# w2, dw2 and the MLP's inner columns on 128 partitions instead of 96

## The chip, the cores and the metric

One core of one Trainium2 chip runs the whole program. The metric is the device time of one execution in microseconds (us); fewer is better. Each comparison ran on one chip, with the kernel before timed in the same rounds. The span of a profile is some 2 us shorter than the time.

## The reference, cut to what matters

The program is a forward pass and its gradient. A gate mixes one decode step of attention with 32 heads over a cache of 4096 keys (A) and an MLP (B). The outputs are the mixed vector and the gradients of nine inputs; only the constant `B_x` gets none.

```python
D, H, Sk, Dh, F = 640, 32, 4096, 128, 1728          # all bfloat16

def _A_ref(x, k_cache, v_cache, wq, wo):
    q = ...(x @ wq)...
    scores = jnp.einsum("bhqd,bhkd->bhqk", q, k_cache) * (Dh ** -0.5)
    p = _softmax(scores, axis=-1)
    o = jnp.einsum("bhqk,bhkd->bhqd", p, v_cache)
    return ...(o)... @ wo

def _B_ref(x, w1, b1, w2):                          # w1 640x1728, w2 1728x640
    h = jnp.einsum("bsd,df->bsf", x, w1) + b1
    sp = jnp.log1p(jnp.exp(-jnp.abs(h))) + jnp.where(h > 0, h, jnp.zeros_like(h))
    act = h * jnp.tanh(sp)
    return jnp.einsum("bsf,fd->bsd", act, w2)

g = _sigmoid((x * gate_w).sum(-1, keepdims=True))
out = g * a + (1 - g) * b
# outputs: out, then the vector-Jacobian product with grad_out for
# x, k_cache, v_cache, wq, wo, w1, b1, w2, gate_w
```

K and V are 33.5 MB each, and so are their gradients. So some four fifths of the traffic (134 of 164.9 MB) are the caches coming in and their gradients going out. w2 is 2.2 MB, and dw2 goes out with as much.

## The kernel before: what the change and the argument touch

All loads but three small rows are issued by SyncE into one queue, and nearly all stores by GpSimd into another. w2 has 1728 rows. Before, each of 96 partitions holds 18 consecutive rows, and three loads bring six of the 18 each. The first two are issued with the loads of the start, and the third mid-run, when a buffer is free.

```python
    FP = 96
    FCN = F // FP            # 18
    FCC = 6
    NCH = FCN // FCC         # 3
    w2_v = B_w2.rearrange("(p fc) n -> p fc n", p=FP)
    dw2_v = out_8.rearrange("(p fc) n -> p fc n", p=FP)
    # ... cut
    def load_w2(c):
        w2cs[c] = mlp.tile([FP, FCC, D], BF16, name="w2c", tag="w2c", bufs=2)
        nc.sync.dma_start(w2cs[c][:], w2_v[:, c * FCC:(c + 1) * FCC, :])

    load_wq(0); load_wo(0); load_k(0); load_v(0); load_k(1); load_v(1); load_wo(1)   # (one per line there)
    nc.sync.dma_start(w1_sb[:], w1_v)
    # ... cut: b1
    load_k(2)
    load_v(2)
    load_w2(0)
    load_w2(1)
```

The work on w2 is one VectorE step for each of the 18 columns of rows in each direction (`dh_part`, `dw2_part`), and five small matmuls for each column for h and again for b:

```python
        def h_part(a, b):  # ... cut
                        nc.tensor.matmul(hps[a][:, fc:fc + 1],
                                         lhsT=w1_sb[:, rc, :].rearrange("p (q c) -> p q c", c=FCN)[:, :, fc],
                                         rhs=x_bf[:, rc:rc + 1], start=(rc == 0), stop=(rc == RC - 1))
        def dh_part(c, i):  # ... cut
                nc.vector.scalar_tensor_tensor(junk[0:FP, 0:D], in0=w2cs[c][:, i, :], scalar=m["dm"][:, fc:fc + 1],
                                               in1=db_bc[0:FP, :], op0=ALU.mult, op1=ALU.mult,
                                               accum_out=m["dh"][:, fc:fc + 1])
```

Two parts of the attention are used by experiments: the sum O over 32 tiles of V in each head, as 32 matmuls with their weight loads (dQ, with K, looks the same), and the last store of all:

```python
            for j in range(a, b):
                nc.tensor.matmul(O, lhsT=vts[h][:, j, :], rhs=st["e"][:, j:j + 1].to_broadcast([P, W]),
                                 start=(j == 0), stop=(j == J - 1))
    # ... cut
    nc.gpsimd.dma_start(dwq_v[:, :, CL:], dwq_l[:])
```

## Time and profile before

The kernel before took 414.11 us, the median of 3 runs (413.64 to 414.41).

| what | where it is read | value |
|---|---|---|
| span | page | 412.1 us |
| bytes moved | page, DMA packets | 164.93 MB |
| VectorE, TensorE busy | page, part 1 | 308.8 us (75%), 305.7 us (74%) |
| DMA in the steady stages | windows | 420 to 422 GB/s, share 1.01 |
| DMA from 28 to 36 us | windows | 291 GB/s, share 1.02 |
| one DMA engine alone at the end | windows | 400 to 408 us |

The windows say more. Each line is a stretch of the span, then its length, the busy time of PE, PEld, DVE, ACT and POOL with counts, then the granted clock, the DMA share and GB/s:

```profile
28.00:36.00 8.00, 7.01 (x165) 6.61 (x165) 5.96 (x14) 4.24 (x10) 1.20 (x2) 1.00 1.02 291
36.00:200.00 164.00, 143.09 (x2726) 132.15 (x2727) 130.04 (x352) 78.25 (x185) 18.27 (x34) 0.98 1.01 421
200.00:280.00 80.00, 55.61 (x1073) 50.08 (x1072) 57.94 (x148) 32.63 (x74) 8.08 (x15) 0.85 1.01 420
304.00:372.00 68.00, 56.36 (x1170) 50.57 (x1168) 61.17 (x150) 35.09 (x80) 10.70 (x17) 1.00 1.01 422
372.00:380.00 8.00, 5.84 (x134) 5.47 (x133) 7.62 (x14) 3.24 (x8) 3.04 (x4) 1.00 0.91 373
380.00:397.00 17.00, 3.42 (x65) 2.30 (x63) 14.85 (x47) 0.79 (x3) 4.73 (x8) 0.59 1.01 417
```

In the three steady stages (36 to 280 and 304 to 372 us) the DMA engines are busy all the time at 420 to 422 GB/s, while the load of the compute engines changes from stage to stage. From 28 to 36 us they are just as busy and move 30% less. The finer windows put this at 30 to 36 us, just where the two early w2 loads are in flight:

```profile
28.00:30.00 2.00, 2.00 (x55) 1.99 (x56) 1.48 (x3) 1.00 (x2) 0.34 (x1) 1.00 1.08 432
30.00:32.00 2.00, 1.47 (x26) 1.35 (x25) 0.55 (x2) 0.67 (x3) 0.32 (x1) 1.00 1.04 254
32.00:34.00 2.00, 1.96 (x38) 1.86 (x36) 2.00 (x3) 2.00 (x5) 0.00 (x0) 1.00 0.99 231
34.00:36.00 2.00, 1.59 (x58) 1.41 (x54) 1.93 (x8) 0.57 (x2) 0.53 (x1) 1.00 1.00 249
```

The end, again by windows, and the closing DRAIN of GpSimd's queue from the view of its source line (durations in ns as min/median/max, then first and last start):

```profile
397.00:400.00 3.00, 0.00 (x0) 0.00 (x0) 0.00 (x0) 0.00 (x0) 0.00 (x0) 0.50 0.76 311
400.00:402.00 2.00, 0.00 (x0) 0.00 (x0) 0.00 (x0) 0.00 (x0) 0.00 (x0) 0.50 0.06 24
404.00:406.00 2.00, 0.00 (x0) 0.00 (x0) 0.00 (x0) 0.00 (x0) 0.00 (x0) 0.50 0.06 27
...
L815 POOLq DRAIN  x3: 45/102/17857, 393.5 to 411.9; - x3
```

A share of 0.06 is one engine of 16. By the landings of the last store, fifteen have ended by 400.5 us and one ends at 407.9 us. The first DRAIN starts at 393.5 us and lasts 17.857 us, so it ends at 411.4 us, 3.5 us after the last store has landed.

### The profile page before, as it was taken

The page shows a single profiled execution, that of the slowest core. Times are in us where ns is not written, and L with a number is a line of the kernel's source. Part 1 is how long each engine was busy: PE and PEld are TensorE (multiplying, and loading weights), DVE is VectorE, ACT ScalarE, POOL GpSimd, SP SyncE. Part 2 cuts the span into 40 slices and gives each one's busy share as a digit, 9 for nine tenths or more (in the row PEclk, how much of TensorE's full clock was granted, in tenths as well). Part 3 has the DMA queues.
Part 4 walks back from the last instruction along what each step waited for, and adds up shares of the span by engine and source line. Part 5 has one row for each costly group of instructions (what it writes and reads, how often), then busy time and mean ns, then how long its engine had stood idle before and what let it go on. Part 6 is the DMA issues. An engine that isn't in the chain of part 4 may idle for free.

```text
span 412.1 us, 13687 instructions
## 1 busy us (share of the span) xinstructions
PE 305.7 (74%) x5916; PEld 277.5 (67%) x5916; DVE 308.8 (75%) x807; ACT 177.0 (43%) x410; POOL 49.9 (12%) x95
## 2 busy tenths in 40 slices
PE   0688899988998789898977688439888788886200
PEld 0577888888887678787867687428777678775200
DVE  3338655685679999999897688528999997978840
ACT  1354534434445455445534356305554555543000
POOL 0001001111110111121111112001111111133310
PEclk9998999999999999989996899958999999999555
DMA  8999999999999999999999999999999999999970
GB/s 292 421 405 336 421 425 415 421 423 425 420 426 422 423 411 415 424 421 422 427 411 425 423 421 419 420 424 393 407 401 428 422 422 421 422 423 383 421 313 14
DMA packets 26328, 164.93 MB, mean 400 GB/s; under 512 B 2812, under 2 KB 2812, under 8 KB 10012
## 3 DMA queue, kind: packets, MB, share of 16 engines
q1 hardware_dynamic: 14116, 82.03, 48.8%
q0 software_dynamic: 12112, 82.03, 47.8%
q8 instruction: 46, 0.75, 0.7%
q14 instruction: 14, 0.11, 0.1%
q10 hardware_dynamic: 40, 0.01, 0.0%
HBM read 82.03 MB, written 82.03 MB: 398 GB/s over the span
## 4 chain that ended last, share of the span: by engine, by line
DVE 33%; PE 30%; DMA 23%; ACT 7%; issue 3%; ACTq 0%; DVEq 0%
DMA Kn<-in_A_k_cache_dram 17%; PE tr L559 10%; DVE dK_sb L584 8%; DVE dV_sb L584 7%; DMA out_dram<-dK_sb 6%; ACT tT L561 6%; PE sA L628 4%; DVE junk L376 4%; PE sA L568 3%; PE h_ps L407 3%; PE sB L681 3%; DVE junk L279 2%; DVE junk L508 2%; PE sB L568 1%; DMA vec_rows<-in_gate_w_dram 1%
## 5 line engine op out<-in xcount | busy, mean ns | idle before, releaser
L561 ACT COPY tT<-tr 128x512 f32<-128x512 f32 x256 | 142.3, 587 | 140.9 <-PE tr L559 140.2
L568 PEld LDWEIGHTS <-tT 128*128 128x128 bf16 x2048 | 80.4, 98 | 40.3 <-ACT tT L561 34.9
L559 PE MATMUL tr<-ident_f,Kn 128*128 128x128 f32 x512 | 80.7, 295 | 6.5 <-DMA Kn<-in_A_k_cache_dram 6.5
L584 DVE TENSOR_TENSOR dV_sb<-p_bf,qd 128x2048 bf16<-128x2048 bf16 x64 | 77.9, 1218 | 2.8 <-DMA out_dram<-dK_sb 2.8
L584 DVE TENSOR_TENSOR dK_sb<-ds_bf,qd 128x2048 bf16<-128x2048 bf16 x64 | 77.7, 1215 | 0.0
L559 PE MATMUL tr<-ident_f,Vn 128*128 128x128 f32 x512 | 72.6, 277 | 0.1
L568 PE MATMUL sA<-qd,tT 128*128 128x48 bf16 x1024 | 48.8, 187 | 23.5 <-ACT dq_all L686 12.8
L559 PEld LDWEIGHTS tr<-ident_f,Kn 128*128 128x128 f32 x512 | 60.1, 150 | 7.6 <-issue 6.2
L559 PEld LDWEIGHTS tr<-ident_f,Vn 128*128 128x128 f32 x512 | 56.8, 143 | 0.2 <-PE sA L568 0.2
L568 PE MATMUL sB<-qd,tT 128*128 128x48 bf16 x1024 | 46.1, 183 | 0.1
L611 POOL DMA_DIRECT2D out_dram<-dV_sb x32 | 18.3, 572 | 166.8 <-DVE dV_sb L584 74.2
L628 PEld LDWEIGHTS <-Vn 128*128 128x128 bf16 x1024 | 30.2, 96 | 10.4 <-issue 10.4
L601 POOL DMA_DIRECT2D out_dram<-dK_sb x31 | 18.3, 591 | 151.0 <-DVE rz L650 77.7
L628 PE MATMUL sA<-e_bf,Vn 128*128 128x48 bf16 x1024 | 30.7, 183 | 7.6 <-DVE zs L648 6.0
L681 PE MATMUL sB<-ds_bf,Kn 128*128 128x48 bf16 x1024 | 31.8, 185 | 3.5 <-DVE ds_bf L670 3.5
L681 PEld LDWEIGHTS <-Kn 128*128 128x128 bf16 x1024 | 29.2, 97 | 3.8 <-issue 3.8
L632 DVE TENSOR_REDUCE m<-sA 128x1 f32<-128x32 f32 x32 | 6.0, 189 | 31.3 <-PE sA L568 25.6
L279 DVE SCALAR_TENSOR_TENSOR junk<-wo_g,da_bc 128x640 bf16<-128x640 bf16 x32 | 26.3, 821 | 2.6 <-ACT da_bc L220 1.1
L376 DVE SCALAR_TENSOR_TENSOR junk<-wq_g,dq_bc 128x1024 bf16<-128x1024 bf16 (+1 forms) x25 | 25.1, 1004 | 0.2
L668 DVE TENSOR_SCALAR_CACHE_REDUCE dj<-sB,rz 128x128 f32<-128x128 f32 x32 | 11.1, 346 | 11.2 <-PE sB L662 11.2
L407 PE MATMUL h_ps<-cols_bf,w_sb 128*96 128x1 bf16 x90 | 18.2, 313 | 1.4 <-ACT qd L290 0.7
L407 PEld LDWEIGHTS <-w_sb 128*96 128x96 bf16 x90 | 17.6, 272 | 1.8 <-issue 0.7
(144 smaller groups left out, 283.8 us busy)
## 6 DMA issues: line engine op xcount, KB each, us to landing
Kn<-in_A_k_cache_dram SPq DMA_DIRECT2D x32, 1024.0 KB, 27.2
Vn<-in_A_v_cache_dram SPq DMA_DIRECT2D x32, 1024.0 KB, 26.9
out_dram<-dV_sb POOLq DMA_DIRECT2D x32, 1024.0 KB, 12.2
out_dram<-dK_sb POOLq DMA_DIRECT2D x31, 1024.0 KB, 12.3
wq_g<-in_A_wq_dram SPq DMA_DIRECT2D x4, 1280.0 KB, 19.0
wo_g<-in_A_wo_dram SPq DMA_DIRECT2D x8, 640.0 KB, 13.3
out_dram<-wo_g POOLq DMA_DIRECT2D x8, 640.0 KB, 11.6
out_dram<-dwq_t POOLq DMA_DIRECT2D x5, 896.0 KB, 16.6
```

The source lines that it names most:

```text
L279: nc.vector.scalar_tensor_tensor(junk[:, 0:D], in0=wos[g][:, i, :], scalar=1.0, in1=da_bc[:], op0=ALU.mult, op1=ALU.mult, accum_out=gp["do ...
L376: nc.vector.scalar_tensor_tensor(junk[:, c0:c1], in0=wqs[w][:, rc, c0:c1], scalar=1.0, in1=dq_bc[:, w * WG * Dh + c0:w * WG * Dh + c1], op ...
L407: nc.tensor.matmul(hps[a][:, fc:fc + 1], lhsT=w1_sb[:, rc, :].rearrange("p (q c) -> p q c", c=FCN)[:, :, fc], rhs=x_bf[:, rc:rc + 1], star ...
L559: nc.tensor.transpose(tp[:, t, :], flat[:, k * P:(k + 1) * P], ident_f[:])
L561: nc.scalar.copy(sb[:].rearrange("p a b -> p (a b)"), tp[:].rearrange("p a b -> p (a b)"))
L568: nc.tensor.matmul(out[:, 2 * k:2 * k + W], lhsT=tb[:, t, par, :], rhs=vec[:, par, :].unsqueeze(1).to_broadcast([P, W // 2, 2]), start=(pa ...
L584: nc.vector.tensor_tensor(dst[:, a:b, :].rearrange("p j (a b) -> p j a b", b=2), col[:, a:b, :].unsqueeze(2).to_broadcast([P, n, Dh // 2, 2]),
L601: nc.gpsimd.dma_start(dKv[h], st["dK"][:])
L611: nc.gpsimd.dma_start(dVv[h], st["dV"][:])
L628: nc.tensor.matmul(O, lhsT=vts[h][:, j, :], rhs=st["e"][:, j:j + 1].to_broadcast([P, W]), start=(j == 0), stop=(j == J - 1))
L668: nc.vector.tensor_scalar(dj[:], PT, rz[:], None, ALU.mult, ALU.add, accum_out=dd[:])
L681: nc.tensor.matmul(DQ, lhsT=kts[h][:, j, :], rhs=ds[:, j, 0:1].to_broadcast([P, W]), start=(j == 0), stop=(j == J - 1))
```

## The change

The intent is to spread w2 and dw2 evenly. 13 rows go on each of 128 partitions (1664 rows), and the 64 rows left over go in a tile of 64 partitions. So 14 columns of work take the place of 18. The diff, cut to its core:

```diff
-    FP = 96
-    FCN = F // FP
-    FCC = 6
-    NCH = FCN // FCC
+    FM = F // P
+    FB = FM * P
+    FR = F - FB
+    FCN = FM + 1
+    CH = [(0, 5), (5, 9), (9, FCN)]
+    NCH = len(CH)
...
-    w2_v = B_w2.rearrange("(p fc) n -> p fc n", p=FP)
-    dw2_v = out_8.rearrange("(p fc) n -> p fc n", p=FP)
+    w2_v = B_w2[0:FB, :].rearrange("(p fc) n -> p fc n", p=P)
+    dw2_v = out_8[0:FB, :].rearrange("(p fc) n -> p fc n", p=P)
...
     def load_w2(c):
-        w2cs[c] = mlp.tile([FP, FCC, D], BF16, name="w2c", tag="w2c", bufs=2)
-        nc.sync.dma_start(w2cs[c][:], w2_v[:, c * FCC:(c + 1) * FCC, :])
+        a, b = CH[c][0], min(CH[c][1], FM)
+        w2cs[c] = mlp.tile([P, 5, D], BF16, name="w2c", tag="w2c", bufs=2)
+        nc.sync.dma_start(w2cs[c][:, 0:b - a, :], w2_v[:, a:b, :])
...
     load_w2(0)
+    w2r = mlp.tile([FR, D], BF16, name="w2r", tag="w2r")
+    nc.sync.dma_start(w2r[:], B_w2[FB:F, :])
     load_w2(1)
...
-                        nc.tensor.matmul(hps[a][:, fc:fc + 1],
-                                         lhsT=w1_sb[:, rc, :].rearrange("p (q c) -> p q c", c=FCN)[:, :, fc],
+                        w = (w1_sb[:, rc, 0:FB].rearrange("p (q c) -> p q c", c=FM)[:, :, fc] if fc < FM
+                             else w1_sb[:, rc, FB:F])
+                        nc.tensor.matmul(hps[a][0:rows(fc), fc:fc + 1], lhsT=w,
...
-    nc.sync.dma_start(out0_rows, fin_rows[0:RC, :])
-    nc.scalar.dma_start(out1_rows, fin_rows[RC:2 * RC, :])
-    nc.sync.dma_start(out9_rows, fin_rows[2 * RC:3 * RC, :])
+    for eng, dst, i, cut in ((nc.sync, out0_rows, 0, 4), (nc.scalar, out1_rows, 1, 3), (nc.sync, out9_rows, 2, 2)):
+        for a, b in ((0, cut), (cut, RC)):
+            eng.dma_start(dst[a:b, :], fin_rows[i * RC + a:i * RC + b, :])
```

Cut: the same split in the b, dh, dw2 and dh-broadcast steps, b1 as two loads, and db1 stored from the broadcast row.

More of the change, by code (lines that the diff above doesn't have):

```diff
@@ L60 @@
     assert Dh == P and J % 8 == 0 and D % P == 0 and H % WG == 0
-    assert F % FP == 0 and FCN % FCC == 0 and FCN % 2 == 0
+    assert 0 < FR <= P and FCN == 14
     Kv = A_k_cache.rearrange("b h (p j) d -> (b h) p j d", p=P)
@@ L72 @@
     dw1_v = out_6.rearrange("(rc r) f -> r rc f", r=P)
-    w2_v = B_w2.rearrange("(p fc) n -> p fc n", p=FP)
-    dw2_v = out_8.rearrange("(p fc) n -> p fc n", p=FP)
-    b1_v = B_b1.rearrange("(p fc) -> p fc", p=FP)
-    db1_v = out_7.rearrange("(p fc) -> p fc", p=FP)
+    w2_v = B_w2[0:FB, :].rearrange("(p fc) n -> p fc n", p=P)
+    dw2_v = out_8[0:FB, :].rearrange("(p fc) n -> p fc n", p=P)
+    b1_v = B_b1[0:FB].rearrange("(p fc) -> p fc", p=P)
     x_rows = A_x.rearrange("a b (c p) -> (a b c) p", p=P)
@@ L148 @@
     nc.sync.dma_start(w1_sb[:], w1_v)
-    b1c = const.tile([FP, FCN], BF16, name="b1c")
-    nc.sync.dma_start(b1c[:], b1_v)
+    b1c = const.tile([P, FCN], BF16, name="b1c")
+    nc.gpsimd.memset(b1c[:], 0.0)
+    nc.sync.dma_start(b1c[:, 0:FM], b1_v)
+    nc.sync.dma_start(b1c[0:FR, FM:FCN], B_b1[FB:F].rearrange("(p c) -> p c", c=1))
     load_k(2)
@@ L397, in mlp_steps, with rows, w2p @@
         m = {}
-        T = lambda name, dt=F32, shape=(FP, FCN): const.tile(list(shape), dt, name=name)
+        T = lambda name, dt=F32, shape=(P, FCN): const.tile(list(shape), dt, name=name)
         b1f = T("b1f")
         hps = {}
+        def rows(fc):
+            return P if fc < FM else FR
+        def w2p(fc):
+            c = [i for i in range(NCH) if CH[i][0] <= fc < CH[i][1]][0]
+            return w2cs[c][:, fc - CH[c][0], :] if fc < FM else w2r[:]
         def h_part(a, b):
             def f():
-                hps[a] = gr_ps.tile([FP, FCN], F32, name="h_ps", tag="gr")
+                hps[a] = gr_ps.tile([P, FCN], F32, name="h_ps", tag="gr")
                 for fc in range(a, b):
                     for rc in range(RC):
-                        nc.tensor.matmul(hps[a][:, fc:fc + 1],
-                                         lhsT=w1_sb[:, rc, :].rearrange("p (q c) -> p q c", c=FCN)[:, :, fc],
+                        w = (w1_sb[:, rc, 0:FB].rearrange("p (q c) -> p q c", c=FM)[:, :, fc] if fc < FM
+                             else w1_sb[:, rc, FB:F])
+                        nc.tensor.matmul(hps[a][0:rows(fc), fc:fc + 1], lhsT=w,
                                          rhs=x_bf[:, rc:rc + 1], start=(rc == 0), stop=(rc == RC - 1))
@@ L416, in f @@
                     m["h"] = T("h_sb")
-                nc.vector.tensor_tensor(m["h"][:, a:b], hps[a][:, a:b], b1f[:, a:b], ALU.add)
+                    nc.gpsimd.memset(m["h"][:], 0.0)
+                r = rows(a)
+                nc.vector.tensor_tensor(m["h"][0:r, a:b], hps[a][0:r, a:b], b1f[0:r, a:b], ALU.add)
             return f
@@ L421, in act1 @@
             h = m["h"]
-            ee = T("ee", shape=(FP, 2, FCN))
+            ee = T("ee", shape=(P, 2, FCN))
             nc.scalar.activation(ee[:, 0, :], h[:], ACT.Exp, scale=1.0)
             nc.scalar.activation(ee[:, 1, :], h[:], ACT.Exp, scale=-1.0)
-            e1 = T("e1", shape=(FP, 2, FCN))
+            e1 = T("e1", shape=(P, 2, FCN))
             nc.vector.tensor_scalar(e1[:], ee[:], 1.0, None, ALU.add)
-            sg = T("sg", shape=(FP, 2, FCN))
+            sg = T("sg", shape=(P, 2, FCN))
             nc.vector.reciprocal(sg[:], e1[:])
@@ L455, in act2 @@
             m["dh"] = T("dh32")
+            nc.gpsimd.memset(m["dh"][:], 0.0)
         def b_part(c):
@@ L460, in f @@
                 for n in range(RC):
-                    for i in range(FCC):
-                        nc.tensor.matmul(m["bp"][:, n:n + 1], lhsT=w2cs[c][:, i, n * P:(n + 1) * P],
-                                         rhs=m["act_bf"][:, c * FCC + i:c * FCC + i + 1],
-                                         start=(i == 0), stop=(i == FCC - 1))
+                    a, b = CH[c]
+                    for fc in range(a, b):
+                        nc.tensor.matmul(m["bp"][:, n:n + 1], lhsT=w2p(fc)[:, n * P:(n + 1) * P],
+                                         rhs=m["act_bf"][0:rows(fc), fc:fc + 1],
+                                         start=(fc == a), stop=(fc == b - 1))
             return f
@@ L468, in b_add, with dh_part, dw2_part @@
             nc.vector.tensor_tensor(b_acc[:], b_acc[:], m["bp"][:], ALU.add)
-        def dh_part(c, i):
+        def dh_part(fc):
             def f():
-                fc = c * FCC + i
-                nc.vector.scalar_tensor_tensor(junk[0:FP, 0:D], in0=w2cs[c][:, i, :], scalar=m["dm"][:, fc:fc + 1],
-                                               in1=db_bc[0:FP, :], op0=ALU.mult, op1=ALU.mult,
-                                               accum_out=m["dh"][:, fc:fc + 1])
+                r = rows(fc)
+                nc.vector.scalar_tensor_tensor(junk[0:r, 0:D], in0=w2p(fc), scalar=m["dm"][0:r, fc:fc + 1],
+                                               in1=db_bc[0:r, :], op0=ALU.mult, op1=ALU.mult,
+                                               accum_out=m["dh"][0:r, fc:fc + 1])
             return f
-        def dw2_part(c, i0, i1):
+        def dw2_part(c, f0, f1):
             def f():
-                for i in range(i0, i1):
-                    fc = c * FCC + i
-                    nc.vector.tensor_scalar(w2cs[c][:, i, :], db_bc[0:FP, :], m["act_f"][:, fc:fc + 1], None, ALU.mult)
-                if i1 == FCC:
-                    nc.gpsimd.dma_start(dw2_v[:, c * FCC:(c + 1) * FCC, :], w2cs[c][:])
+                for fc in range(f0, f1):
+                    r = rows(fc)
+                    nc.vector.tensor_scalar(w2p(fc), db_bc[0:r, :], m["act_f"][0:r, fc:fc + 1], None, ALU.mult)
+                if f1 == CH[c][1]:
+                    a, b = CH[c][0], min(f1, FM)
+                    nc.gpsimd.dma_start(dw2_v[:, a:b, :], w2cs[c][:, 0:b - a, :])
+                    if f1 == FCN:
+                        nc.gpsimd.dma_start(out_8[FB:F, :], w2r[:])
             return f
@@ L491, in dh_cast @@
             nc.vector.tensor_copy(m["dh_bf"][:], m["dh"][:])
-            nc.gpsimd.dma_start(db1_v, m["dh_bf"][:])
             m["dh_bc"] = mlp.tile([P, F], BF16, name="dh_bc", tag="dh_bc")
@@ L496, in f @@
             def f():
-                ps = gr_ps.tile([P, hc, FP], BF16, name="dhb_ps", tag="gr")
+                ps = gr_ps.tile([P, hc, P], BF16, name="dhb_ps", tag="gr")
                 for i in range(hc):
-                    nc.tensor.transpose(ps[:, i, :], m["dh_bf"][:, k * hc + i:k * hc + i + 1].to_broadcast([FP, P]),
-                                        ident_bf[0:FP, 0:FP])
-                nc.scalar.copy(m["dh_bc"][:].rearrange("p (q c) -> p q c", c=FCN)[:, :, k * hc:(k + 1) * hc],
-                               ps[:].rearrange("p c q -> p q c"))
+                    fc = k * hc + i
+                    r = rows(fc)
+                    nc.tensor.transpose(ps[:, i, 0:r], m["dh_bf"][0:r, fc:fc + 1].to_broadcast([r, P]),
+                                        ident_bf[0:r, 0:r])
+                n = min(hc, FM - k * hc)
+                nc.scalar.copy(m["dh_bc"][:, 0:FB].rearrange("p (q c) -> p q c", c=FM)[:, :, k * hc:k * hc + n],
+                               ps[:, 0:n, :].rearrange("p c q -> p q c"))
+                if k == 1:
+                    nc.scalar.copy(m["dh_bc"][:, FB:F], ps[:, n, 0:FR])
+                    nc.gpsimd.dma_start(out_7.rearrange("(o f) -> o f", o=1), m["dh_bc"][0:1, :])
             return f
@@ L528, in mlp_steps @@
             add(f"badd{c}", "T", b_add, (f"b{c}",), H0)
-            for i in range(FCC):
-                add(f"dh{c}_{i}", "D", dh_part(c, i), ("act2", f"w2_{c}"), H0)
-            add(f"dw2a_{c}", "D", dw2_part(c, 0, 3), (f"badd{c}",) + tuple(f"dh{c}_{i}" for i in range(FCC)), H0)
-            add(f"dw2_{c}", "D", dw2_part(c, 3, 6), (f"dw2a_{c}",), H0)
+            a, b = CH[c]
+            for fc in range(a, b):
+                add(f"dh_{fc}", "D", dh_part(fc), ("act2", f"w2_{c}"), H0)
+            add(f"dw2a_{c}", "D", dw2_part(c, a, a + 3), (f"badd{c}",) + tuple(f"dh_{fc}" for fc in range(a, b)), H0)
+            add(f"dw2_{c}", "D", dw2_part(c, a + 3, b), (f"dw2a_{c}",), H0)
             if c < 2:
@@ L542, in mlp_steps @@
                         (f"w2x{k - 1}_{c}" if k else f"w2l_{c}",), H0)
-        add("dhc", "T", dh_cast, (f"dh{NCH - 1}_{FCC - 1}",), H0)
+        add("dhc", "T", dh_cast, (f"dh_{FCN - 1}",), H0)
         add("dhb0", "P", dh_bc_part(0), ("dhc",), H0)
```

## The prediction

> **What bounds the kernel now.** The DMA engines, almost everywhere. The table by stages has 421 GB/s at a busy share of 1.01 from 36 to 200 us, 420 from 200 to 280 and 422 from 304 to 372; 164.93 MB at 421 GB/s are 392 of the 412.1 us span. VectorE (75%) and TensorE (74%) have gaps; the chain of waits runs through them for long stretches, yet has two waits for a K load of 34.7 and 33.6 us (from 197.7 and 242.9 us) and one of 23.4 us for a store. Compute that runs ahead is given back there. At the end a DMA share of 0.06 (25 GB/s) remains from 400 to 408 us: one engine of 16 finishes some 8 us late.
>
> So what counts is where the DMA is below 421 GB/s: the start (256 to 8 us), 28 to 36 us, 280 to 304 us (397), 372 to 380 us (373), and the tail. From 28 to 36 us it moves 291 GB/s although the share is 1.02: (421-291)/421 x 8 = 2.5 us lost. There the first two w2 loads run (96 partitions, 720 KB each), with hardly a store beside them.
>
> **Why there.** The Trainium skill, "SBUF — State Buffer", section "Door 1: The DMA port swizzle", says that partitions 0 to 63 reach only the 8 even SBUF ports, 64 to 127 the odd ones. A 96-partition tile then puts two thirds of its bytes on half the ports. The trace agrees: busy engines, few bytes, just there. The third w2 load (about 212 to 227 us, mixed with stores) shows no such dip (406 to 425 GB/s), so the gain is from the first two.
>
> **What the change removes, adds, moves.**
> - DMA: equal bytes. The two early w2 loads go on 128 partitions: up to 2.5 us back. New: a 64-partition load of 82 KB (0.2 us more than balanced, estimate), a few hundred small packets, three more final row stores: under 0.2 us.
> - VectorE: 18 to 14 steps of 0.87 + 0.08 us and of 0.38 us: 5.3 us less.
> - TensorE: 20 of 90 h and 20 of 90 b matmuls go. The h weight loads (272 ns for 96 strided columns) grow to about 360 ns (estimate by columns), so h stays near 25 us; b saves 2 us.
> - The MLP ends earlier: its dw1 store leaves one or two heads earlier.
>
> On the critical path: the 2.5 us of DMA, because the queues have a backlog from then on (loads land 14 to 35 us after issue). The compute saved I count at nearly nothing: it lengthens waits for loads. The last small stores end before the late engine, so splitting them should not show.
>
> **Time.** 414.1 - 2.5 + 0.2 - 0.3 (something from compute) = 411.5 us, range 408.8 to 413.9. Chances: faster by over 2% 0.05, within 2% 0.93, slower by over 2% 0.02.
>
> **What would show it.** From 28 to 36 us the rate should be 400 GB/s or more, with the next K load landing about 2.5 us earlier. Later stages should keep 420 GB/s; VectorE should be some 5 us less busy, and the long K waits not shorter. The tail with one late engine should remain, 7 to 9 us long.
>
> **What would make it wrong.** If compute really sets 36 to 200 us, VectorE's 5 us count, and the gain is up to 6 us. If the late DMA engine sets the end and was not slowed at 28 to 36 us, the gain is near 0. If the moved dw1 store leaves DMA idle at the end, or the extra small loads hold back the load queue, it can be slower.

("The start (256 to 8 us)" in it means 256 GB/s from 0 to 8 us.)

## More of the kernel before

From the page of the kernel before: the busy time of each engine, the DMA queue that brings instructions, and the two heads of the chain of waits that ended last (shares of the span by engine, then by line):

```profile
PE 305.7 (74%) x5916; PEld 277.5 (67%) x5916; DVE 308.8 (75%) x807; ACT 177.0 (43%) x410; POOL 49.9 (12%) x95
...
q8 instruction: 46, 0.75, 0.7%
...
DVE 33%; PE 30%; DMA 23%; ACT 7%; issue 3%; ACTq 0%; DVEq 0%
DMA Kn<-in_A_k_cache_dram 17%; PE tr L559 10%; DVE dK_sb L584 8%; DVE dV_sb L584 7%; DMA out_dram<-dK_sb 6%; ACT tT L561 6%; PE sA L628 4%; DVE junk L376 4%; PE sA L568 3%; PE h_ps L407 3%; PE sB L681 3%; DVE junk L279 2%; DVE junk L508 2%; PE sB L568 1%; DMA vec_rows<-in_gate_w_dram 1%
```

The chain spreads over VectorE, TensorE and DMA. Its shares alone do not say which resource sets the time.

## The result, and the profile after

The changed kernel took 413.45 us, the median of 6 runs (413.24 to 413.93). The kernel before took 414.26 us in the same rounds, the median of 6 runs (413.64 to 414.88). The ratio is 0.9983, with a 95% interval of 0.9970 to 0.9996. Here and below, a ratio is the mean time of one kernel's runs over the mean of the other's in the same rounds, so it is not quite the ratio of the medians quoted. The gain is 0.8 us by the medians, where 2.6 us were predicted. The time lies inside the predicted range, at its upper end. Later rounds (`after_again`) gave less still: 0.9993.

The page of the changed kernel, the same parts as before:

```profile
PE 296.3 (72%) x5872; PEld 268.2 (65%) x5872; DVE 303.1 (74%) x791; ACT 177.1 (43%) x411; POOL 50.8 (12%) x99
...
q8 instruction: 46, 0.75, 0.7%
...
DMA 38%; DVE 33%; PE 19%; ACT 4%; issue 3%; POOL 0%; ACTq 0%; SPq 0%; POOLq 0%; DVEq 0%
DMA Kn<-in_A_k_cache_dram 30%; PE tr L586 8%; DVE dK_sb L611 7%; DVE dV_sb L611 7%; DMA out_dram<-dV_sb 6%; DVE junk L382 4%; ACT tT L588 3%; PE sA L655 3%; DVE junk L285 3%; PE sA L595 2%; PE sB L708 2%; DVE junk L534 1%; DVE junk L491 1%; DMA vec_rows<-in_gate_w_dram 1%; DVE dj L695 1%
```

VectorE is 5.7 us less busy and TensorE 9.4 us. In the chain, DMA takes 38% instead of 23%, and the K loads alone 30% instead of 17%: what compute saved shows as longer waits for loads. The windows of the changed kernel, where they can be set against those of before:

```profile
28.00:36.00 8.00, 7.06 (x175) 6.66 (x170) 5.96 (x16) 4.23 (x11) 1.20 (x2) 1.00 1.02 395
36.00:200.00 164.00, 130.08 (x2632) 118.56 (x2633) 124.57 (x333) 76.91 (x181) 18.05 (x35) 0.95 1.01 422
304.00:372.00 68.00, 53.31 (x1117) 48.17 (x1117) 58.07 (x145) 32.51 (x75) 10.88 (x17) 0.98 0.99 412
372.00:380.00 8.00, 7.46 (x106) 7.06 (x107) 5.74 (x11) 3.74 (x8) 2.06 (x3) 0.77 1.00 399
380.00:397.00 17.00, 4.99 (x122) 3.87 (x119) 15.60 (x45) 1.79 (x6) 5.78 (x8) 0.67 0.97 385
...
30.00:32.00 2.00, 1.47 (x27) 1.36 (x25) 0.72 (x2) 0.84 (x3) 0.15 (x1) 1.00 1.05 409
32.00:34.00 2.00, 1.96 (x36) 1.77 (x35) 2.00 (x4) 2.00 (x5) 0.00 (x0) 1.00 1.02 337
...
404.00:406.00 2.00, 0.00 (x0) 0.00 (x0) 0.00 (x0) 0.00 (x0) 0.00 (x0) 0.50 0.06 26
```

The slow stretch is nearly gone: 395 GB/s instead of 291. Only 32 to 34 us, where the new 64-partition load runs, is still at 337. From 304 to 372 us and from 380 to 397 us the rate is lower than before (412 for 422, 385 for 417), from 372 to 380 us it is higher (399 for 373), and the one late engine is still there at the end.

One side effect was not foreseen in this size. The views of the tiles `w_sb` show the weight loads of the h matmuls, the kernel before first and the changed kernel second:

```profile
L407 PEld LDWEIGHTS <-w_sb x90: 252/277/279, 47.8 to 119.7; 128*96 128x96 bf16 x90
```

```profile
L422 PEld LDWEIGHTS <-w_sb x70: 106/158/169, 45.2 to 100.4; 128*128 128x128 bf16 x65, 128*64 128x64 bf16 x5
```

A weight load of 128 columns that lie 13 elements apart takes a median of 158 ns, and one of 96 columns 18 apart took 277 ns. The number of columns and their distance changed together, so these two do not say which of them matters. The h matmuls took 5.9 us of TensorE instead of 18.2.

To see where the early gain went, the landings of the slowest engine's share of single DMAs were read from the trace, each in us from the start of the span. This is a calculation from the DMA completion records. A second trace of each kernel is in it, from the control runs described below:

```
last landing of          before  before, 2nd   after  after, 2nd
V of head 2               33.6      33.8        32.0     32.2
K of head 3               45.3      45.7        43.8     43.4
V of head 20             247.0     247.8       245.4    245.9
K of head 31             365.0     364.8       364.6    364.5
last store (dwq)         407.9     408.6       407.5    407.3
```

Early on, the changed kernel is 1.4 to 2.3 us ahead by the slowest engine in every pairing. At the K load of head 31 it is 0.2 to 0.5 us ahead. Two traces of one kernel differ by up to 0.8 us, so a difference of 1 us between two single traces is no firm ground. Two more cautions: loads share the engines with stores, whose order differs between the two kernels; and the engine that is slowest early need not be the one that is late at the end. In the first trace of the kernel before, no engine is late at the K load of head 5: its fifteenth and its last share both land at 62.4 us.

### The profile page after: what moved, and what is told of

Same layout as the page of the kernel before. It is cut to its first block, busy times and chain, and to the rows that moved or that the text cites. A ratio compares the mean times of both kernels' runs of the same rounds, so it can differ in the third digit from the quotient of the medians.

```text
span 411.8 us, 13602 instructions
## 1 busy us (share of the span) xinstructions
PE 296.3 (72%) x5872; PEld 268.2 (65%) x5872; DVE 303.1 (74%) x791; ACT 177.1 (43%) x411; POOL 50.8 (12%) x99
## 4 chain that ended last, share of the span: by engine, by line
DMA 38%; DVE 33%; PE 19%; ACT 4%; issue 3%; POOL 0%; ACTq 0%; SPq 0%; POOLq 0%; DVEq 0%
DMA Kn<-in_A_k_cache_dram 30%; PE tr L586 8%; DVE dK_sb L611 7%; DVE dV_sb L611 7%; DMA out_dram<-dV_sb 6%; DVE junk L382 4%; ACT tT L588 3%; PE sA L655 3%; DVE junk L285 3%; PE sA L595 2%; PE sB L708 2%; DVE junk L534 1%; DVE junk L491 1%; DMA vec_rows<-in_gate_w_dram 1%; DVE dj L695 1%
## 5 line engine op out<-in xcount | busy, mean ns | idle before, releaser
L586 PE MATMUL tr<-ident_f,Kn 128*128 128x128 f32 x512 | 82.2, 299 | 6.5 <-DMA Kn<-in_A_k_cache_dram 6.5
L586 PEld LDWEIGHTS tr<-ident_f,Kn 128*128 128x128 f32 x512 | 61.6, 153 | 7.7 <-issue 5.2
L586 PEld LDWEIGHTS tr<-ident_f,Vn 128*128 128x128 f32 x512 | 55.9, 141 | 0.0
L638 POOL DMA_DIRECT2D out_dram<-dV_sb x32 | 18.2, 569 | 170.2 <-DVE dV_sb L611 58.5
L275 PE MATMUL qc_ps<-cols_bf,wq_g 128*128 128x1 bf16 x160 | 5.3, 164 | 22.1 <-DMA wq_g<-in_A_wq_dram 22.1
L275 PEld LDWEIGHTS <-wq_g 128*128 128x128 bf16 x160 | 4.8, 100 | 22.6 <-DMA wq_g<-in_A_wq_dram 22.4
```

What stands on the lines that cost most here:

```text
L275: nc.tensor.matmul(qc_ps[:, hh:hh + 1], lhsT=wq[:, rc, off + hh * Dh:off + (hh + 1) * Dh], rhs=x_bf[:, rc:rc + 1], start=(rc == 0), stop=( ...
L586: nc.tensor.transpose(tp[:, t, :], flat[:, k * P:(k + 1) * P], ident_f[:])
L638: nc.gpsimd.dma_start(dVv[h], st["dV"][:])
```

## The experiments

The theory after the result was: the end of the run is set by the late DMA engine; compute does not matter; the early gain must then be lost on the way, or it never was a gain for the end. The rivals were that compute sets the time after all, that the split small stores or the new 64-partition load cost what was gained, and that a gain made early is simply worth less than one made late.

### What the late engine carries: half_o and plus_o

The queue of instructions moved 46 packets and 0.75 MB, which is 16 KB each. Both kernels below start from the changed kernel. In half_o every second product of O and dQ is left out, and with it 2048 of TensorE's instructions (matmuls and weight loads). In plus_o the products of the even tiles are done twice. Their outputs are wrong, which doesn't matter for the times.

```diff
-            for j in range(a, b):
+            for j in range(a, b, 2):            # half_o; stop at J - 2; the same for dQ
```

```diff
             for j in range(a, b):
+                for k in range(2 - j % 2):      # plus_o; start only at k == 0; the same for dQ
```

> The changed kernel with the O and dQ sums over every second tile only: 1,024 matmuls and 1,024 weight loads less (wrong results on purpose), bytes of tensors equal. Theory L (one late DMA engine, which also carries TensorE's instruction fetches of 16 KB, 46 in all, sets the time): 8 fetches less, each worth 0.35 to 0.6 us of that engine (16 KB at its 26.5 GB/s would be 0.62): 3 to 5 us faster than the changed kernel (ratio to before about 0.986 to 0.991), and the last store's late engine lags less than 5.6 us. Rival P (all 16 DMA engines alike set the time, the late one is an effect of the tail): within 0.5 us of the changed kernel. Rival C (compute sets the time): 1 to 6 us faster from less TensorE work.

> The changed kernel with every second tile of the O and dQ sums multiplied twice: 1,024 matmuls and 1,024 weight loads more (wrong results on purpose). Theory L: 8 fetches of 16 KB more on the late DMA engine, 3 to 5 us slower than the changed kernel, and the late engine's lag at the end grows from 5.6 us by about as much. Rival P: within 0.5 us. Rival C: slower too, by up to the added TensorE time (2048 instructions at about 30 ns each per pair: up to 30 us where TensorE is in the chain), with the lag of the late engine unchanged or smaller.

half_o took 410.5 us (410.18 to 410.95, 4 runs), a ratio of 0.9921 (0.9906 to 0.9936). plus_o took 416.92 us (416.75 to 417.42), a ratio of 1.0077 (1.0062 to 1.0092). The pages show the queue of instructions, half_o first:

```profile
q8 instruction: 38, 0.62, 0.6%
```

```profile
q8 instruction: 54, 0.88, 0.8%
```

By means that is 3.3 us less and 3.2 us more than before. Against the changed kernel, from which both were made and which is some 0.5 us faster than before (see the control runs below), eight packets fewer come with 2.8 us less (3 to 5 were expected) and eight more with 3.7 us more: 0.35 and 0.46 us per packet. The last engine's last landing moved by -3.7 and +3.5 us. 2048 instructions in 8 packets of 16 KB are 64 bytes each.

These two kernels also change TensorE's busy time (275.0 and 318.2 us), and one expectation failed: the lag of the late engine behind the fifteenth in the last store was to shrink in half_o and to grow by 3 to 5 us in plus_o. It is 6.3 and 5.7 us, against 5.6 and 6.5 in the two traces of the changed kernel. An unchanged lag in plus_o is what the rival "compute" had announced. Landings in the middle of the run tell the two apart better. These are the shares of the V load of head 20, in us, read as in the table above:

```
                       half_o  changed  changed, 2nd  plus_o
fifteenth engine        237.8   238.6      238.5       238.4
last engine             243.4   245.4      245.9       248.4
```

The fifteenth engine is where it was within 0.8 us; the last one alone is 2.0 us and more earlier with fewer packets and 2.5 to 3.0 us later with more. A slower or faster TensorE gives no reason for one engine alone to move. That all the packets go to that engine remains an inference, since the records do not name the engine; the later stages, where the other engines move too, are not taken apart here.

### Does compute set the time: short_dx

The 25 products for dx on wq of the changed kernel are cut to 32 of their columns. This is wrong, though the missing share of dx is so small that the comparison with the reference passes.

```diff
-                nc.vector.scalar_tensor_tensor(junk[:, c0:c1], in0=wqs[w][:, rc, c0:c1], scalar=1.0,
-                                               in1=dq_bc[:, w * WG * Dh + c0:w * WG * Dh + c1],
+                nc.vector.scalar_tensor_tensor(junk[:, c0:c0 + 32], in0=wqs[w][:, rc, c0:c0 + 32], scalar=1.0,
+                                               in1=dq_bc[:, w * WG * Dh + c0:w * WG * Dh + c0 + 32],
```

> The changed kernel with the 25 products for dx from wq cut from 1,024 (512) columns to 32 (wrong dx on purpose): about 20 us of VectorE work less, the same number of instructions and the same bytes. Theory L and rival P (DMA sets the time): within 1 us of the changed kernel, VectorE busy 280 to 285 us in place of 303. Rival C: faster by 3 us or more.

VectorE's busy time fell from 303.1 to 283.6 us, and the time was 413.3 us (413.14 to 413.4), a ratio of 0.9988 (0.9973 to 1.0002). That is where the changed kernel stands without it. Twenty microseconds less of the busiest compute engine are worth nothing that shows here. So the 5.7 us that the change saves on VectorE, though in other places of the run, are not likely to count either.

### The early loads moved away: w2_later

The kernel before, with the first two w2 loads issued at heads 2 and 4 instead of at the start.

```diff
     load_v(2)
-    load_w2(0)
-    load_w2(1)
...
         load_v(h + 3)
+        if h in (2, 4):
+            load_w2(h // 2 - 1)
```

> The kernel before, with its first two w2 loads (96 partitions) issued at heads 2 and 4 in place of at the start, so that they run beside stores. If the ports of a lopsided tile slow only a stretch without stores, the dip at 28 to 36 us (291 GB/s) goes, no new one appears, and the time falls like that of the changed kernel: 0.5 to 2 us (ratio 0.995 to 0.999). If the gain of the changed kernel came from less compute, this one is like before (within 0.3 us).

It took 413.37 us (412.27 to 413.94), a ratio of 0.9983 (0.9963 to 1.0004), which leaves open whether it gained. The windows show where the slow stretch went:

```profile
28.00:36.00 8.00, 7.22 (x174) 6.86 (x174) 5.92 (x14) 4.37 (x11) 1.20 (x2) 1.00 1.01 423
36.00:60.00 24.00, 21.37 (x379) 19.77 (x377) 17.13 (x48) 11.98 (x29) 2.13 (x4) 1.00 1.02 411
60.00:80.00 20.00, 18.43 (x327) 17.43 (x324) 11.40 (x32) 9.18 (x22) 2.11 (x4) 1.00 1.01 401
80.00:100.00 20.00, 17.94 (x328) 16.88 (x324) 14.09 (x42) 7.71 (x18) 2.14 (x5) 0.91 1.01 411
```

The dip at 28 to 36 us is gone, and shallower ones stand at 36 to 100 us instead (before: 419 to 423 there). The expectation that no new dip would come was a miss. The reading in the prediction, that a 96-partition load does not dip beside stores because the third one showed nothing, was not general. Against 421 GB/s the three new dips are 24 x 10/421 + 20 x 20/421 + 20 x 10/421 = 2.0 us of rate, not much less than the 2.5 us of the old dip. Finer windows place them at the two loads: 353 and 334 GB/s from 56 to 60 and 60 to 64 us, where the first load lands (58 to 63 us), and 372 GB/s from 88 to 92 us, where the second begins to land (89 to 97 us).

### A control and two small parts: after_again, tail_sp, fin_whole

after_again is the changed kernel once more. tail_sp has the last store issued by SyncE (it is the control for tail_k4 below). fin_whole does not split the last row stores.

```diff
-    nc.gpsimd.dma_start(dwq_v[:, :, CL:], dwq_l[:])
+    nc.sync.dma_start(dwq_v[:, :, CL:], dwq_l[:])          # tail_sp
```

```diff
-    for eng, dst, i, cut in ((nc.sync, out0_rows, 0, 4), ...):     # fin_whole: the three stores of before
+    nc.sync.dma_start(out0_rows, fin_rows[0:RC, :])
+    nc.scalar.dma_start(out1_rows, fin_rows[RC:2 * RC, :])
+    nc.sync.dma_start(out9_rows, fin_rows[2 * RC:3 * RC, :])
```

> The changed kernel once more, for a tighter interval and a second trace: ratio to before 0.9965 to 0.9985 (0.6 to 1.5 us faster). If the late DMA engine keeps all that it gained by 48 us (1.5 us), the lower end; if it loses most of it again, the upper.

> Control for tail_k4: the changed kernel with its last store (dwq_l, 640 KB, 128 partitions) issued from SyncE in place of GpSimd, still over all 16 DMA engines. Every theory: within 0.5 us of the changed kernel.

> The changed kernel with the three final row stores whole again, as before. All theories: within 0.4 us of the changed kernel, because the rows are stored before the late engine ends its own queue.

after_again: 413.35 us (413.25 to 413.72, 5 runs), 0.9993 (0.9979 to 1.0006), above the 0.9965 to 0.9985 that were expected. tail_sp: 413.5 us (412.88 to 413.61), 0.9992 (0.9979 to 1.0004). fin_whole: 413.23 us (413.07 to 413.55, 4 runs), 0.9990 (0.9976 to 1.0003). Neither part shows, so the split stores are not what ate the gain. With the first result and w2r_late below, five kernels that differ in nothing that shows give 0.9983, 0.9993, 0.9992, 0.9990 and 0.9981, on average 0.9988: the gain is about 0.5 us.

### Taking the late engine out of one store: tail_k4

The last store of the changed kernel goes as 124 and 4 partitions instead of 128.

```diff
-    nc.gpsimd.dma_start(dwq_v[:, :, CL:], dwq_l[:])
+    nc.sync.dma_start(dwq_v[0:124, :, CL:], dwq_l[0:124])
+    nc.sync.dma_start(dwq_v[124:P, :, CL:], dwq_l[124:P])
```

The idea rests on the Trainium skill, "DMA: Bandwidth & Descriptors", section "Why a DMA increments its semaphore by 16 and not by 1": a DMA uses the largest number of engines up to 16 that divides its outer dimension, so 124 rows go on 4 engines, and from SyncE these are the lowest-numbered ones. Which ones they were, no run here shows; that the late engine was not among them is read from its earlier end. The trace agrees with the number of four: each of the two stores has five completion increments, one at once and four as data lands.

> The last store (dwq_l, 640 KB) as two DMAs of 124 and 4 partitions from SyncE. The Trainium skill says that such a DMA is spread over the largest number up to 16 that divides its rows, here 4, and on the lowest-numbered engines. Theory L with the late engine not among those four: the late engine is spared 40 KB, 1.5 us at 26.5 GB/s; the four get 120 KB more each, 4.5 us, and have 5.6 to 7.4 us to spare: 1.2 to 1.5 us faster than tail_sp. If the late engine is among the four: 4 to 5 us slower. Rival P (all 16 alike): 1.5 us faster for twelve, later for four: 3 us slower or more.

It took 411.55 us (411.29 to 412.2), a ratio of 0.9951 (0.9938 to 0.9963), and so 1.7 us less than its control tail_sp (0.41% of 413.8 us). The windows of tail_k4:

```profile
400.00:402.00 2.00, 0.00 (x0) 0.00 (x0) 0.00 (x0) 0.00 (x0) 0.00 (x0) 0.50 0.32 113
404.00:406.00 2.00, 0.00 (x0) 0.00 (x0) 0.00 (x0) 0.00 (x0) 0.00 (x0) 0.50 0.26 91
406.00:408.00 2.00, 0.00 (x0) 0.00 (x0) 0.00 (x0) 0.00 (x0) 0.00 (x0) 0.50 0.06 15
```

The windows of its control tail_sp:

```profile
400.00:402.00 2.00, 0.00 (x0) 0.00 (x0) 0.00 (x0) 0.00 (x0) 0.00 (x0) 0.50 0.09 34
404.00:406.00 2.00, 0.00 (x0) 0.00 (x0) 0.00 (x0) 0.00 (x0) 0.00 (x0) 0.50 0.07 27
```

Now about five engines (0.32 of 16) work where one did, and the late engine lands its last share of GpSimd's stores at 405.2 us instead of 406.8. The row stores, which wait behind the four engines' larger shares, now land last, at 408.7 us. The same bytes, spread so that the late engine has fewer, shorten the run. TensorE's instructions are unchanged. So the late engine's load does set the end.

### Is early time worth less than late time: skip_early and skip_late

The changed kernel without its second w2 load (655 KB, at the start), and without its third (655 KB, issued at 165 us). The tile is filled by a memset; both are wrong.

```diff
-        nc.sync.dma_start(w2cs[c][:, 0:b - a, :], w2_v[:, a:b, :])
+        if c != 1:                                             # skip_early; c != 2 in skip_late
+            nc.sync.dma_start(w2cs[c][:, 0:b - a, :], w2_v[:, a:b, :])
```

> The changed kernel without its second w2 load (128 partitions, 655 KB, at the start, landing by 39 us); the tile is filled by GpSimd (wrong results on purpose). 41 KB per DMA engine, 1.5 us at 27 GB/s, are spared before 40 us, as the change spared 1.5 us there. If DMA time spared early counts in full at the end: 1.5 us faster than the changed kernel. If most of it is lost again on the way (the reading of the changed kernel's traces): 0.2 to 0.8 us.

> The same with the third w2 load in its place (also 655 KB, issued at 165 us): the same bytes, spared in the stretch in which the late DMA engine falls behind. Theory L: 1.5 us faster than the changed kernel, more than skip_early. If early and late count alike, both are the same within 0.4 us.

skip_early took 411.68 us (411.64 to 411.78), a ratio of 0.9941 (0.9928 to 0.9953); skip_late 411.73 us (411.5 to 412.32), 0.9943 (0.9930 to 0.9957). By means, that is 2.4 and 2.3 us less than before, and 1.9 and 1.8 us less than the changed kernel (which is at -0.5). At 421 GB/s, 655 KB are 1.6 us. So bytes taken away count in full, early as late. The theory that every early gain is lost on the way falls.

### What a lopsided load costs the end: bskip_early and bskip_late

The same in the kernel before, whose loads are 737 KB on 96 partitions. If the shape costs the end what the slow stretch suggests, some 1.15 to 1.25 us for each of the two loads, leaving one out must gain that on top of its bytes.

```diff
-        nc.sync.dma_start(w2cs[c][:], w2_v[:, c * FCC:(c + 1) * FCC, :])
+        if c != 1:                                             # bskip_early; c != 2 in bskip_late
+            nc.sync.dma_start(w2cs[c][:], w2_v[:, c * FCC:(c + 1) * FCC, :])
```

> The kernel before without its second w2 load (737 KB on 96 partitions, among the start's loads; wrong values on purpose). In the changed kernel 655 KB taken away early was worth 1.9 us, so 737 KB at full pace are worth 2.1 us. If the lopsided shape costs the end of the run what the slow stretch suggests (2.3 us for two loads, half of it for one), the gain is 3.2 us: ratio 0.9922. If the lopsided shape costs the end nearly nothing, because the late DMA engine is not among those that it overloads, or because the time is made good later, the gain is 2.1 us: ratio 0.995.

> The kernel before without its third w2 load (737 KB on 96 partitions, mid-run beside the stores; wrong values on purpose). Same two theories: 3.2 us, ratio 0.9922, if a lopsided load costs the end about 1.1 us more than its bytes; 2.1 us, ratio 0.995, if it doesn't. If early and late differ, the place matters.

bskip_early took 411.93 us (411.45 to 412.51, 6 runs), a ratio of 0.9946 (0.9932 to 0.9959); bskip_late 412.39 us (411.7 to 413.0, 6 runs), 0.9956 (0.9943 to 0.9969). By means, the gains are 2.2 and 1.9 us, with intervals of 1.7 to 2.8 and 1.3 to 2.4 us. The ratio of 0.9922, for a shape that costs 1.1 us more, is outside both intervals; 0.9950, for bytes alone, is inside both. Per megabyte the lopsided loads are worth 3.0 and 2.5 us, the level ones of skip_early and skip_late 2.9 and 2.7. At the end of the run, the shape of one such load costs nothing that these runs can resolve. The slow stretch was real all the same: with one of the two loads gone, the windows of bskip_early show 329 GB/s where before had 291:

```profile
28.00:36.00 8.00, 6.97 (x165) 6.57 (x165) 5.96 (x16) 4.20 (x10) 1.20 (x2) 1.00 1.02 329
```

This line also limits what the test says. Only (329 - 291)/421 x 8 = 0.7 us of the 2.5 us of rate came back, not half of it, and the third load showed no slow stretch to begin with. A cost of 1.15 us for each load does not fit the intervals; one of 0.7 us for this load, on top of its bytes, is not excluded. The stronger test of the whole stretch is w2r_late, below.

The trace of bskip_early also warns against reading a landing as time gained. Its K load of head 3 lands at 41.1 us, 4.2 us earlier than in the first trace of before, though the run gains about half of that. Loads share the engines with stores from 30 us on. A load that runs at half the rate and is left out moves the next one by twice its own time; this is an argument that fits the numbers, not a measurement.

### The new small load: w2r_late, with before_again as control

The changed kernel with its 64-partition load issued at head 3; and the kernel before, unchanged, for a second trace.

```diff
     load_w2(0)
     w2r = mlp.tile([FR, D], BF16, name="w2r", tag="w2r")
-    nc.sync.dma_start(w2r[:], B_w2[FB:F, :])
     load_w2(1)
...
         load_v(h + 3)
+        if h == 3:
+            nc.sync.dma_start(w2r[:], B_w2[FB:F, :])
```

> The changed kernel with its 64-partition load of w2 (82 KB) issued at head 3 rather than between the two w2 loads of the start. If that small load is what holds the stretch at 32 to 34 us at 337 GB/s, and that costs the end in full (2 us at 337 rather than 420 GB/s, 0.4 us), the time falls by 0.3 to 0.4 us: ratio 0.998 of before. If it doesn't count, the ratio stays at 0.999.

> The kernel before, unchanged, as a control: ratio 1.000 within 0.0015. Its trace is compared with the first one: if the late DMA engine's landings at 48 us and at the end vary by more than 0.5 us between two traces of one kernel, the difference of 1 us that I read from single traces is not safe to explain.

w2r_late took 413.55 us (412.77 to 413.68, 5 runs), 0.9981 (0.9967 to 0.9994). before_again took 414.05 us (413.12 to 414.67, 6 runs), 0.9998 (0.9983 to 1.0012). The windows of w2r_late have no slow stretch left:

```profile
28.00:36.00 8.00, 7.24 (x174) 6.83 (x174) 5.96 (x14) 4.31 (x11) 1.20 (x2) 1.00 1.02 420
```

So the small load was what held 32 to 34 us at 337 GB/s. What its removal from there is worth is not resolved against the changed kernel's 0.9983 and 0.9993. The expectation of 0.998 came out, but so would the rival's 0.999: both lie in the interval. The run shows something more important: the slow stretch is gone altogether (420 GB/s), and the gain on before is 0.8 us, with an interval of 0.2 to 1.4 us. The 2.5 us by which the stretch was priced lie outside it.

### What the end really waits for: tail_hw and tail_hw_k4

In tail_hw every store of the changed kernel from dwo of group 6 on is issued by SyncE instead of GpSimd, because GpSimd's closing DRAIN ended 3.5 us after the last landing. tail_hw_k4 also sends that dwo as 124 and 4 partitions.

```diff
-            nc.gpsimd.dma_start(dwo_v[g], wos[g][:])
+            (nc.sync if g >= NG - 2 else nc.gpsimd).dma_start(dwo_v[g], wos[g][:])          # tail_hw
...                                                    # and so for dK, dV, dwq of the last heads and dwq_l
```

```diff
+            if g == NG - 2:                           # tail_hw_k4 only
+                nc.sync.dma_start(dwo_v[g][0:124], wos[g][0:124])
+                nc.sync.dma_start(dwo_v[g][124:P], wos[g][124:P])
```

> The changed kernel with all stores from dwo of group 6 on (about 362 us) issued by SyncE in place of GpSimd. In the traces so far GpSimd's closing drain ends 3.5 us after its own last store lands; where SyncE issued the store that landed last (tail_k4), the program ended 1.0 us after it. Expected: the last landing stays (within 0.7 us), the drain is over before it, and the program is about 3 us faster than the changed kernel (ratio to before about 0.991).

> tail_hw with the store of dwo of group 6 (640 KB) as 124 and 4 partitions, so on four DMA engines that are not the late one. Theory L: 1 to 1.6 us faster than tail_hw (ratio to before about 0.987), more than tail_k4 by the drain. Rival P: no better than tail_hw.

tail_hw took 410.1 us (409.88 to 410.76), a ratio of 0.9905 (0.9890 to 0.9920). tail_hw_k4 took 408.25 us (407.73 to 408.57, 4 runs), 0.9856 (0.9841 to 0.9871): 2.0 us less than tail_hw by means, where 1 to 1.6 were expected. Its results are correct, and it is faster than both kernels. The DRAIN lines of tail_hw and of the changed kernel, in this order:

```profile
L842 POOLq DRAIN  x3: 45/102/29682, 359.9 to 408.1; - x3
```

```profile
L842 POOLq DRAIN  x3: 45/102/17834, 393.2 to 411.5; - x3
```

In tail_hw the long DRAIN ends at 359.9 + 29.7 = 389.6 us, well before the last landing at 407.3 us, and the span of 408.3 us ends 1.0 us after that landing. In the changed kernel the DRAIN ends at 411.0 us, the last landing is at 407.5 us, and the span of 411.8 us ends 4.3 us after it. The difference of 3.3 us is what tail_hw gains on the changed kernel (3.9 us by means on before, less the 0.5 of the change: 3.4). tail_sp, which moved one store only, gained nothing, because the stores left on GpSimd still ended last on the late engine (406.8 us).

The kept traces agree without exception. In the fifteen in which GpSimd issued the stores that landed last, the span ends 4.26 to 4.30 us after the last landing; in tail_k4, tail_hw and tail_hw_k4, where SyncE issued it, 0.97 to 1.03 us after it. So in the first fifteen the time is that of the late engine's last landing plus a constant.

## Why the prediction was wrong in size

- **That the DMA engines set the time: right.** 20 us less VectorE work (short_dx) were worth nothing that shows, and bytes taken away counted in full (1.8 to 1.9 us for 655 KB).
- **That 28 to 36 us is slow because of the 96-partition loads, and that the change mends it: right.** 291 became 395 GB/s (400 were predicted), and 420 with the small load moved away as well. The cause named is the one in the Trainium skill, "SBUF — State Buffer", section "Door 1: The DMA port swizzle": partitions 0 to 63 reach only half the SBUF ports. The traces agree in kind: the slow stretch went when the tiles were filled, moved when the loads were moved (w2_later), and what was left of it went with the 64-partition load. That it is the ports, and not something else about a tile on part of the partitions, no run here separates. In size it is worse than a plain reading: if the 64 lower partitions of 96 set the pace at half of 421 GB/s, the tile would move at 3/4 of the full rate, 316 GB/s (an estimate), and 231 to 254 were measured.
- **"On the critical path: the 2.5 us of DMA, because the queues have a backlog from then on": this step failed.** 2.5 us was the rate lost by all 16 engines together, taken as time lost at the end. The end belongs to one engine (tail_k4, and the constant 4.3 us from its last landing to the end). The K load of head 3 landed 1.5 us earlier on the slowest engine (2.3 us in the second traces), not 2.5. At the end the gain is about 0.5 us, and 0.8 (0.2 to 1.4) where the slow stretch is gone altogether (w2r_late). Taking one of the lopsided loads out agrees: it gains 2.2 or 1.9 us, its bytes, and not the 3.2 us of bytes and lost rate. A level load of 737 KB would be worth 2.1 us (2.9 us per MB, from skip_early), so the shape of one load measures 0.1 and -0.2 us at the end, with some 0.9 us of uncertainty either way (both runs have their interval), where the prediction had booked 1.25 for each of two.
- **The warning was in the text.** "If the late DMA engine sets the end and was not slowed at 28 to 36 us, the gain is near 0." Its first half is what tail_k4 shows. The second half is not settled: the engine that was slowest early was slowed, by 1.4 to 2.3 us in the traces, but whether it is the one that is late at the end the records do not say, and most of the lead was not kept. In the landings, the lead of the loads shrinks between 248 and 365 us. Why stays open: skip_early shows that DMA time spared early need not be lost. In the same stretch the changed kernel moves less (412 GB/s from 304 to 372 us, where before had 422); whether that is a cause, or only the other 15 engines running out of work earlier, no run here separates.
- **Compute counts nearly nothing: right as far as tested** (VectorE by short_dx; TensorE's 9 us have no run of their own), and the h weight loads were wrong without harm: 158 ns each instead of the estimated 360. That the long K waits would not get shorter also held: K loads rose from 17% to 30% of the chain.
- **Small terms: right.** The split row stores (fin_whole) and the small load (w2r_late) do not show in the time.
- **"Later stages should keep 420 GB/s": wrong.** 422 became 412 from 304 to 372 us and 417 became 385 from 380 to 397 us, though 373 became 399 from 372 to 380 us.
- **The tail of one late engine remains: right**, but 5.6 us long (6.5 in the second trace) instead of 7 to 9.

## What to carry to other kernels

A stretch in which the DMA engines are busy and move fewer bytes is a lead, not yet a gain: ask which engine ends last and price the stretch by what that one loses, or simply leave the load out and time it. When a share of 1/16 remains for microseconds at the end, give that engine less (fewer instruction fetches, as half_o suggests, or a last store on other engines, as tail_k4 shows) rather than making the average faster. And look at what runs after the last landing: here moving the last stores from GpSimd to SyncE was worth 3.4 us, and the change itself 0.5.

## What the Trainium skill lacked or had wrong

- "DMA: Bandwidth & Descriptors" has nothing on instruction fetches as a load on one DMA engine. Here TensorE's instructions come in 46 packets of 16 KB; against the changed kernel, eight fewer went with 2.8 us less and eight more with 3.7 us more (half_o, plus_o), and mid-run one engine alone moved with them.
- "Runtime: NRT & Kernel Launch", section "Instruction fetch mechanics", calls the cost of crossing a 16 KiB boundary of instructions "one DMA tail-bump, mostly hidden". The trace agrees with the size of the packets (46 of 16 KB), but here the time moved with their number, by 0.35 to 0.46 us each (half_o, plus_o; both changed TensorE's work too).
- No page that I found has the wait at the end of a kernel whose last stores were issued by GpSimd: its DRAIN ended 3.5 us after the last landing, and the span 4.3 us after it (fifteen traces), against 1.0 us with the last stores on SyncE (tail_hw).
- "SBUF — State Buffer", section "Door 1: The DMA port swizzle", explains 64 partitions but gives no figure for 96. Measured: 231 to 254 GB/s in windows where the 96-partition loads run, 421 in level stages. It does not warn that this need not reach the end of a run in full (w2r_late: 2.5 us of rate regained, 0.8 us of time).
- No page that I found gives the time of a weight load whose columns lie apart: here 277 ns for 96 columns 18 elements apart, 158 ns for 128 columns 13 apart (number and distance changed together).
